# Value rows of the first token block: one-kilobyte loads put in order by 0/1 matmuls, with a new instruction order

## The chip, the cores and the metric

The kernel runs on one core of a Trainium2 chip. A core has a matrix engine (TensorE, PE in the profile; its weight loads are listed apart as PEld), three engines for elementwise work (VectorE, DVE; ScalarE, ACT; GpSimd, POOL), and SyncE (SP), which here only issues DMA transfers. The metric is the device time of one execution in microseconds. Three runs of the kernel before gave 293.53, 294.14 and 294.15 us; the median is 294.14 us.

## The reference

Attention within chunks of 64 tokens, then a bilinear feed-forward layer. q, k and v are float32 of shape (8, 8, 576, 64): batch, head, token, head dimension.

```python
def _attn_ref(q, k, v):
    B, H, S, D = q.shape                      # 8, 8, 576, 64
    chunk = 64
    q_c, k_c, v_c = (x.reshape(B, H, S // chunk, chunk, D) for x in (q, k, v))
    scores = (1.0 / np.sqrt(D)) * np.matmul(q_c, k_c.transpose(0, 1, 2, 4, 3))
    scores = scores - np.max(scores, axis=-1, keepdims=True)
    attn = np.exp(scores)
    attn = attn / (np.sum(attn, axis=-1, keepdims=True) + 1e-09)
    return np.matmul(attn, v_c).reshape(B, H, S, D)

def _moe_ref(x, w_a, w_b, w_out):             # x: 4608 tokens x 512
    a = x @ w_a                               # 512 x 1536
    b = x @ w_b
    return a * b @ w_out                      # 1536 x 512
```

Between the two, the heads of a token are joined: x is the attention's output as 4608 rows of 512.

## The kernel before

**Tiling.** The 4608 tokens are nine blocks of 512, numbered K = 0 to 8, and each block is two units of 256 tokens, u = 0 to 17. A block's attention output stands in the tile `xT` (features on partitions, tokens along the free axis). The feed-forward layer of a block multiplies `xT` with the weights `WA` and `WB` (twelve pieces `ft` of 128 columns each), multiplies the two results into `AB`, and multiplies `AB` with `WO`. From block 1 on, the two products use seven half-size products instead of eight (`side_group`, L832 and its product at L861; `out_seven`, L1135 and L1166; the last block's is `out_last`, L1004). Block 0's first product is plain (`ffn`, L762, product at L772).

**Attention of block 0.** It is done in quarters: head pairs m = 0 to 3, two heads of all 512 tokens each. `load_pair` (L364) loads q and k of one pair; partition p holds the four tokens 4p to 4p + 3 of a head one after the other, so that each contiguous run in memory is 4 x 64 float32, one kilobyte. `cast_pair` makes bf16 of it, `turn_pair` (L480, matmuls at L492) transposes it on TensorE and copies it back from PSUM in token order (`qkT`), `scores_pair` (L506, matmuls at L518, exponentials to `E` at L528), `sums_pair` (L533, matmuls with ones at L541; the inverse on DVE with a reciprocal at L551 for pair 1, on ACT as exp(-ln) at L555 and L557 for the others) and `values_pair` (L560, matmuls at L570, the multiplication with the inverse into `xT` at L583).

**v of block 0.** The value product needs v with the token on the partition. `load_v0` (L373) loads it so: four transfers, each of 128 tokens, all eight heads; a run in memory is one token of one head, 64 float32, 256 bytes. Two casts (`cast_v`, L592) turn the two float32 halves into the bf16 tiles `vb[0]` and `vb[1]`, 128 x 1024 each. All four `values_pair` wait for both casts.

**Units 2 and 3** (block 1) are loaded and turned in the same way (`TWO_UNITS`); their v comes by `load_v0(..., 1)`, in 256-byte runs. Later units are loaded in token order and turned by a DMA transpose (`turn_dma`, L602).

**Weights.** `load_four` loads 256 rows by 512 columns of `w_a` or `w_b` (512 KB, runs of two kilobytes) into one of eight staging tiles `wst`, and a cast writes them to `WA` or `WB`. There are twelve such loads, X0, X1 and X2, four each. `load_wo` does the same for `w_out`.

**Order.** Nothing is scheduled while the kernel is built. Each piece of work is an operation with a number, the engines that may do it, and what it reads and writes (`Planner.op`, L25). The text `ORDER_OF_ALL` (L85) lists all operations in one order, each with the engine that does it (a PE, b ACT, c DVE, d POOL, e SP) and, where it takes one, the PSUM bank. `follow` (L53) emits them in that order. Each engine works through its own part of the list strictly in order; only semaphores between engines tell when. Words with f are filler matmuls of zeros (L1474) that write a free bank and are read by nobody; there are 30. Transfers are issued by SP, and the k pairs of block 0 by ACT's queue, and share a set of completion semaphores, eight transfers deep: a transfer is issued when the one eight before it has landed. Some POOL operations also wait for the DVE operation listed just before them (the `turn` dependency at the end of the kernel).

## Time and profile before

| | |
|---|---|
| median of three runs | 294.14 us (293.53 to 294.15) |
| span of the profiled execution, first to last instruction | 291.4 us |
| PE busy | 285.0 us (98%), 3522 matmuls |
| DVE busy | 245.6 us (84%) |
| ACT busy | 181.5 us (62%) |
| POOL busy | 175.3 us (60%) |
| DMA | 55.09 MB in 140248 packets, mean 189 GB/s |
| first product of block 0's feed-forward layer (L772) | starts at 16.28 us |
| first product of block 1 (L861) | starts at 42.94 us |

The profile gives the span of one execution; its own device time is not given apart from that. The median of the runs is 2.7 us above the span, which is what lies before the first and after the last instruction. The profile counts matmuls with modelled ends, so that "busy" on PE also covers short waits between them; the time from the start of one group of matmuls to the start of the next tells more than their listed duration. Times in the profile are counted from the first instruction.

### The profile page before, as it was taken

How to read it: one execution, taken by the hardware profiler on the slowest of the kernel's cores; microseconds unless marked ns; L12 is line 12 of the kernel's file. 1: busy time of each engine (PE TensorE's matmuls, PEld its weight loads, DVE VectorE, ACT ScalarE, POOL GpSimd, SP SyncE). 2: the span in 40 equal slices, each digit the busy share in tenths (PEclk: the TensorE clock that was granted, in tenths of full speed). 3: DMA queues.
4: the chain of work that ended last, by engine and by line, in shares of the span. 5: the costliest groups of instructions: out<-in, count | busy, mean ns of one | idle time of the engine just before them, and what ended most of it. 6: DMA issues, size and time to landing. Idle time of an engine off the chain costs nothing.

```text
span 291.4 us, 8635 instructions
## 1 busy us (share of the span) xinstructions
PE 285.0 (98%) x3522; PEld 232.6 (80%) x3522; DVE 245.6 (84%) x432; ACT 181.5 (62%) x308; POOL 175.3 (60%) x168
## 2 busy tenths in 40 slices
PE   8999989999999999999999999999999999999995
PEld 3545448887888888888888888888888888888884
DVE  2758989999897999989998989888997788697893
ACT  1767878978877775795675468525944684333221
POOL 3354248443789389835739694569447764676540
PEclk9999999999999999999999999999999999999999
DMA  7999999999998789939996995939290210003034
GB/s 244 335 395 393 310 282 340 246 216 246 213 213 219 191 175 274 240 75 201 260 259 158 203 277 126 253 88 242 76 219 3 80 69 2 0 2 144 3 133 156
DMA packets 140248, 55.09 MB, mean 189 GB/s; under 512 B 126256, under 2 KB 131504, under 8 KB 140208
## 3 DMA queue, kind: packets, MB, share of 16 engines
q1 hardware_dynamic: 138976, 53.43, 71.8%
q10 hardware_dynamic: 1232, 1.11, 1.1%
q8 instruction: 27, 0.44, 0.7%
q14 instruction: 13, 0.11, 0.1%
HBM read 37.75 MB, written 9.44 MB: 162 GB/s over the span
## 4 chain that ended last, share of the span: by engine, by line
PE 91%; ACT 3%; DVE 2%; DMA 1%; issue 1%; POOL 0%; SPq 0%; POOLq 0%
PE F L861 49%; PE F L1166 24%; PE F L772 6%; PE F L1004 3%; PE F L1474 2%; PE F L635 1%; PE F L645 1%; PE F L492 1%; PE F L673 1%; DMA f<-in_k_dram 1%; ACT inv L697 1%; ACT inv L695 1%; DVE xT L722 0%; POOL wst L821 0%; ACT E L528 0%
## 5 line engine op out<-in xcount | busy, mean ns | idle before, releaser
L326 ACT COPY part<-F 128x512 f32<-128x512 f32 x87 | 50.4, 591 | 49.0 <-PE F L861 32.2
L895 POOL TENSOR_TENSOR AB<-AB,bsb 128x512 bf16<-128x512 bf16 x45 | 51.7, 1156 | 38.7 <-DVE wst L1123 15.5
L899 DVE TENSOR_TENSOR bsb<-F,part 128x512 bf16<-128x512 f32 x72 | 49.0, 685 | 10.4 <-PE F L861 4.9
L326 ACT COPY wst<-F 128x512 f32<-128x512 f32 (+1 forms) x43 | 24.0, 561 | 30.5 <-PE F L861 14.7
L861 PEld LDWEIGHTS <-WB 128*128 128x128 bf16 x384 | 37.3, 98 | 5.2 <-issue 0.5
L861 PEld LDWEIGHTS <-WA 128*128 128x128 bf16 x384 | 37.2, 98 | 4.8 <-issue 0.3
L899 DVE TENSOR_TENSOR AB<-F,part 128x512 bf16<-128x512 f32 x48 | 32.9, 686 | 3.7 <-PE F L861 1.6
L1123 POOL TENSOR_TENSOR wst<-AB 128x512 bf16<-128x512 bf16 x27 | 31.0, 1155 | 7.0 <-PE F L1166 4.7
L861 PEld LDWEIGHTS <-Ta 128*128 128x128 bf16 x288 | 27.9, 98 | 3.9 <-issue 0.5
L861 PEld LDWEIGHTS <-Tb 128*128 128x128 bf16 x288 | 27.4, 98 | 4.4 <-issue 0.9
L1166 PEld LDWEIGHTS <-AB 128*128 128x128 bf16 x288 | 28.0, 98 | 3.4
L1166 PEld LDWEIGHTS <-wst 128*128 128x128 bf16 x288 | 27.8, 98 | 3.4
L861 PE MATMUL F<-wst,Ta 128*128 128x256 bf16 x192 | 28.8, 273 | 0.1
L861 PE MATMUL F<-wst,Tb 128*128 128x256 bf16 x192 | 28.8, 273 | 0.0
L861 PE MATMUL F<-wst,WB 128*128 128x256 bf16 x192 | 28.8, 273 | 0.0
L861 PE MATMUL F<-wst,WA 128*128 128x256 bf16 x192 | 28.8, 273 | 0.0
L861 PE MATMUL F<-xT,WA 128*128 128x256 bf16 x192 | 28.2, 273 | 0.0
L861 PE MATMUL F<-xT,WB 128*128 128x256 bf16 x192 | 28.1, 273 | 0.0
L1166 PE MATMUL F<-WO,AB 128*128 128x256 bf16 x192 | 25.5, 273 | 0.0
L326 DVE COPY part<-F 128x512 f32<-128x512 f32 x33 | 22.4, 684 | 2.7 <-PE F L861 2.0
L326 ACT CAST qkb<-f 128x1024 bf16<-128x1024 f32 (+1 forms) x24 | 23.2, 986 | 0.3 <-DMA f<-in_q_dram 0.3
L1123 POOL TENSOR_TENSOR wst<-wst,AB 128x512 bf16<-128x512 bf16 x16 | 18.4, 1155 | 6.0 <-DVE wst L1123 5.9
(126 smaller groups left out, 551.7 us busy)
## 6 DMA issues: line engine op xcount, KB each, us to landing
f<-in_q_dram SPq DMA_DIRECT2D x32, 256.0 KB, 4.2
f<-in_v_dram SPq DMA_DIRECT2D x32, 256.0 KB, 4.2
f<-in_k_dram SPq DMA_DIRECT2D x28, 256.0 KB, 4.8
out_dram<-osb SPq DMA_DIRECT2D x28, 256.0 KB, 3.5
wst<-in_moe_w_b_dram SPq DMA_DIRECT2D x6, 512.0 KB, 7.8
wst<-in_moe_w_a_dram SPq DMA_DIRECT2D x6, 512.0 KB, 6.9
wst<-in_moe_w_out_dram SPq DMA_DIRECT2D x6, 512.0 KB, 6.8
out_dram<-osb SPq DMA_DIRECT2D x12, 128.0 KB, 2.4
```

Source lines behind the costliest of these rows:

```text
L326: return A.copy(out=out, in_=in_) if e == "act" else ENG[e].tensor_copy(out=out, in_=in_)
L492: T.transpose(turned()[:, r, :], qkb[hu][:, x, mm * 512 + r * 128:mm * 512 + r * 128 + 128], identity)
L635: T.matmul(PS[j][cl * 64:cl * 64 + 64, c:c + 64], chunk_of(u, 1, m, j, 2 * g + cl), chunk_of(u, 0, m, j, 2 * g + cl), start=True, stop=True,)
L645: T.matmul(SU[cl][j * 64:j * 64 + 64, :], ones[cl * 64:cl * 64 + 64, :], E[u % 2][cl * 64:cl * 64 + 64, j, :], start=True, stop=True,)
L772: T.matmul(f_of(b)[:, 0:n].rearrange("p (u t) -> p u t", u=len(us)), w[ft][:, kt, :], x[:, us[0]:us[-1] + 1, kt, :], start=(kt == 0), stop ...
L861: T.matmul(f_of(bank)[:, q * 256:q * 256 + 256], lhs(2 * g + q, kt), rhs[:, kt, :], start=(first and q == 0 and kt == 0), stop=(q == 1 and ...
L895: op(("dve", "pool"), TIMES, lambda e: ENG[e].tensor_tensor(out=dst, in0=dst, in1=b, op=MULT), r=bk, w=key, prio=-300, fast=True)
L899: op("dve", c_dve(512), lambda e: V.tensor_tensor(out=dst, in0=two(f_of(bank)), in1=two(pab[s][i]), op=ADD), r=[("ps", id(bank)), ("part", ...
L1004: T.matmul(f_of(bank)[:, 0:256], lhs[:, i, h], rhs[:, i, :], start=(first and i == 0), stop=(i == NP - 1), skip_group_check=True)
L1123: op(*long_op(hs), lambda e, i=i, x=x, y=y, o_=o_: ENG[e].tensor_tensor(out=SS[i][:, s], in0=x[:, s], in1=y[:, s], op=o_), r=fts + [(name, ...
L1166: T.matmul(f_of(bank)[:, at:at + 256], lhs[:, i, tt * 128:tt * 128 + 128], rhs[:, i, :], start=(first and at == 0 and i == 0), stop=(i == ...
L1474: "fn": lambda e: T.matmul(F[at], zero[:, 0:128], zero, start=True, stop=True),
```

## The change

Three things are changed.

1. `load_v0` of block 0 (`K in PLACED`) loads v by head pairs, as q and k are loaded: four transfers of 256 KB in runs of one kilobyte, four tokens on a partition.
2. `place_v` brings it into token order. For each half (four heads), two copies cast 128 x 512 float32 to bf16 into a part of the output tile `osb[0]` that is not yet in use, with the four residues r of the token index apart. Sixteen matmuls then put the rows in place: the stationary operand is a 32 x 128 piece of `picks`, a matrix of zeros with a one where column - 3 equals four times the partition, and the moving operand is a 32 x 256 piece of v. Four are accumulated over r for each of four 32-row groups g, which write four PSUM banks. Four copies of 128 x 256 bring these to `vb`. The keys of `vb` are now kept apart by half, so that pairs 0 and 1 wait for the first half only. `picks` (128 x 515 bf16, in `osb[2]`) is made at the start by a memset and a select on GpSimd. The two `cast_v` of block 0 are gone.
3. `ORDER_OF_ALL` is another table, for all operations of the kernel. It was made for three sets of transfer times. Operation numbers differ between the tables. In the new one the first weight load comes after the q, k and v loads of block 0 and three of the q and k loads of units 2 and 3 (before: none of these three), all twelve weight loads come before the v loads of units 2 and 3 (before: two of these four v loads came ahead of the last two weight loads), and there are 25 fillers.

```diff
--- before.py
+++ after.py
@@ -83,95 +83,90 @@
 ORDER_OF_ALL = """
-c113 e0 b1 e2 b3 e4 e8 b5 e6 e9 c48 f0 f1 f2 f3 f4 f5 f6 f7 f0 f1 a49:0 c50 d51 f2 a52:1 d57 f3 f4 a58:2 b7
...
+c125 e0 b1 e2 d48 b3 e4 b5 e6 d57 b51 b7 f0 f0 f0 f0 f0 f0 f0 f0 a52:0 a49:1 a58:2 b59 c60 a61:3 b62 f4 f4 f4 f4
...
 """
@@ -247,6 +242,9 @@
     SUMS_AT = 12
     EARLY_CASTS = ("pool", "act", "dve")
     TWO_CASTS = ("pool", "act", "dve")
+    PLACED = (0,)
+    BY_HALF = (0,)
+    PLACE_CASTS = ("pool", "act", "dve")
 
     sb = ctx.enter_context(tc.tile_pool(name="sb", bufs=1))
     pp = ctx.enter_context(tc.tile_pool(name="pp", bufs=1, space=bass.MemoryType.PSUM))
@@ -317,6 +315,8 @@
     TS[0] = WO[:, :, 0, 256:512]
     TW = [[W[:, 1::2, 0:2]] + [buf(f"T{x}_{i}", [128, NP, 2, 128], BF16) for i in range(3)] for x, W in (("b", WB), ("a", WA))]
 
+    picks = osb[2].rearrange("p t c -> p (t c)").bitcast(BF16)[:, 0:515]
+
     V, A, G, T, SP = nc.vector, nc.scalar, nc.gpsimd, nc.tensor, nc.sync
     P = Planner({"F": range(NF)})
     op = P.op
@@ -371,6 +371,15 @@
         ))
 
     def load_v0(half, K=0):
+        if K in PLACED:
+            for m in (2 * half, 2 * half + 1):
+                mm = m % 2
+                load(
+                    f32[half][2][:, mm * 512:mm * 512 + 512].rearrange("p (h c) -> p h c", h=2),
+                    v[K, 2 * m:2 * m + 2, 0:BLK, :].rearrange("h (p r) d -> p h (r d)", r=4),
+                    [("f32", half, 2, 2 * mm), ("f32", half, 2, 2 * mm + 1)], (256, 42),
+                )
+            return
         for n in range(2):
             g = 2 * half + n
             load(
@@ -574,7 +583,7 @@
                             start=True, stop=True,
                         )
 
-        op("pe", 0.157, pe, r=[("E", hu, mm, j) for j in range(2)] + [("vb", 0), ("vb", 1)], w=[("ps", id(x)) for x in PA], ps=PA, prio=R0 + m + 0.4, mode="64")
+        op("pe", 0.157, pe, r=[("E", hu, mm, j) for j in range(2)] + [("vb", n, g, hu) for n in range(2) for g in range(2)], w=[("ps", id(x)) for x in PA], ps=PA, prio=R0 + m + 0.4, mode="64")
         if MERGE and not mm:
             return
         a, n = (hu * 2, 2) if MERGE else (m, 1)
@@ -589,9 +598,50 @@
                    w=[("xT", 0, u, y, cl) for u in range(2) for y in range(a, a + n)], ps=[PA[cl]], prio=R0 + m + 0.4)
             o["ahead"] = AHEAD * (1 - hu)
 
+    def vb_keys(n):
+        return [("vb", n, g, h) for g in range(2) for h in range(2)]
+
     def cast_v(u, engs, prio):
         cost = {"dve": 0.69, "pool": 1.04, "act": 1.05}
-        op(engs, [cost[e] for e in engs], lambda e: copy(e, vb[u % 2], f32[u % NF32][2]), r=f_keys(u, 2), w=[("vb", u % 2)], prio=prio, fast=True)
+        op(engs, [cost[e] for e in engs], lambda e: copy(e, vb[u % 2], f32[u % NF32][2]), r=f_keys(u, 2), w=vb_keys(u % 2), prio=prio, fast=True)
+
+    def v_rows(K, half):
+        return osb[K].rearrange("p t c -> p (t c)").bitcast(BF16)[:, half * 1024:half * 1024 + 1024]
+
+    placing = {}
+
+    def place_v(K, half):
+        cost = {"dve": 0.425, "pool": 0.61, "act": 0.62}
+        rows = v_rows(K, half)
+        for mm in range(2):
+            op(PLACE_CASTS, [cost[e] for e in PLACE_CASTS], lambda e, mm=mm: copy(
+                e,
+                rows.rearrange("p (r h d) -> p r h d", r=4, h=4)[:, :, 2 * mm:2 * mm + 2],
+                f32[half][2][:, mm * 512:mm * 512 + 512].rearrange("p (h r d) -> p r h d", h=2, r=4),
+            ), r=[("f32", half, 2, 2 * mm), ("f32", half, 2, 2 * mm + 1)], w=[("osb", K, half, mm)], prio=R0, fast=True)
+        if K in BY_HALF or not half:
+            placing[K] = [P.bank("F") for _ in range(4)]
+            keep.extend(placing[K])
+        VB = placing[K]
+
+        def pe(e):
+            for r in range(4):
+                for g in range(4):
+                    T.matmul(
+                        f_of(VB[g])[:, half * 256:half * 256 + 256],
+                        picks[32 * g:32 * g + 32, 128 * g + 3 - r:128 * g + 131 - r],
+                        rows[32 * g:32 * g + 32, r * 256:r * 256 + 256],
+                        start=(r == 0), stop=(r == 3), skip_group_check=True,
+                    )
+
+        op("pe", 0.441, pe, r=[("osb", K, half, mm) for mm in range(2)] + [("osb", 2, 0, 0), ("osb", 2, 0, 1)], w=[("ps", id(b)) for b in VB], ps=VB, prio=R0, mode="32")
+        if K in BY_HALF or half:
+            for g in range(4):
+                hs = (half,) if K in BY_HALF else (0, 1)
+                c = slice(256 * hs[0], 256 * hs[-1] + 256)
+                n = 256 * len(hs)
+                op(("act", "dve"), (c_act(n), c_dve(n)), lambda e, g=g, c=c: copy(e, vb[g // 2][:, g % 2 * 512:g % 2 * 512 + 512][:, c], f_of(VB[g])[:, c]),
+                   r=[("ps", id(VB[g]))], w=[("vb", g // 2, g % 2, h) for h in hs], ps=[VB[g]], prio=R0)
 
 
     def cast_natural(u, x, engs, prio):
@@ -726,7 +776,7 @@
                     op=MULT,
                 ), r=[("ps", id(PA[cl]))] + i_keys(u), w=[("xT", (u // 2) % NX, u % 2, m, cl) for m in range(4)], ps=[PA[cl]], prio=prio)
 
-        return 0.256, lambda: mm_values(u, [f_of(x) for x in PA]), e_keys(u) + [("vb", n) for n in ((0, 1) if u in TWO else (u % 2,))], PA, old, post
+        return 0.256, lambda: mm_values(u, [f_of(x) for x in PA]), e_keys(u) + ([("vb", n, g, u % 2) for n in range(2) for g in range(2)] if u in TWO else vb_keys(u % 2)), PA, old, post
 
     def part_scores(u, prio):
         PS = P.bank("F"), P.bank("F")
@@ -1313,8 +1363,11 @@
             cast_pair(x, m, PAIR_CASTS[2 * m + x])
             turn_pair(m, x, PAIR_TURNS[2 * m + x])
         scores_pair(m)
-    cast_v(0, V_CASTS, R0 + 0.4)
-    cast_v(1, V_CASTS, R0 + 0.5)
+    for half in range(2):
+        if 0 in PLACED:
+            place_v(0, half)
+        else:
+            cast_v(half, V_CASTS, R0 + 0.4)
     for m in range(2):
         sums_pair(m)
         values_pair(m)
@@ -1343,7 +1396,9 @@
 
     def value_in(u):
 
-        if u < NU:
+        if u in TWO and 1 in PLACED:
+            place_v(1, u % 2)
+        elif u < NU:
             cast_v(u, EARLY_CASTS if u < 8 else CASTS, -60 + u)
 
     AT = -200.0
@@ -1476,6 +1531,8 @@
     with tc.manual_schedule():
         V.memset(ones, 1.0)
         make_identity(nc, identity)
+        G.memset(picks, 0.0)
+        G.affine_select(out=picks, in_=picks, pattern=[[-1, 515]], compare_op=mybir.AluOpType.not_equal, fill=1.0, base=3, channel_multiplier=4)
         tables, turn = False, None
         for o in order:
             if o["eng"] == "act" and not o["land"] and not tables:
```

171 lines of the change are left out of this document (83 added, 88 removed).

## The prediction

> **What bounds the kernel now.** I read the page first (its shares and the 40 slices), then the busy time of the dense stretch, then the chain of work that ended last, and then the timeline of the first 45 us. The page:
>
> ```profile
> span 291.4 us, 8635 instructions
> ...
> PE 285.0 (98%) x3522; PEld 232.6 (80%) x3522; DVE 245.6 (84%) x432; ACT 181.5 (62%) x308; POOL 175.3 (60%) x168
> ...
> GB/s 244 335 395 393 310 282 340 246 216 246 213 213 219 191 175 274 240 75 201 260 259 158 203 277 126 253 88 242 76 219 3 80 69 2 0 2 144 3 133 156
> ```
>
> The table of busy time by stretch, 42 to 250 us (PE busy first):
>
> ```profile
> 42.00:250.00 208.00, 207.85 (x2710) 179.65 (x2708) 186.40 (x327) 140.57 (x228) 137.32 (x124) 1.00 0.79 183
> ```
>
> PE is busy for 207.85 of 208 us. From 42 us on it sets the time, and a change gains nothing there unless it takes PE work away. Of PE work the change takes none: it adds 32 small matmuls and drops five fillers. What can move is how early the dense part starts. The chain that ended last (start, length, work):
>
> ```profile
> 16.28 5.89 PE F L772 x26
> 22.39 4.75 PE F L772 x22
> 27.14 0.67 PE F L492 x12
> ...
> 28.70 0.62 PE F L492 x8
> 29.75 0.86 PE F L772 x4
> ...
> 41.27 1.83 PE F L772 x8
> 43.11 9.61 PE F L861 x88
> ```
>
> and PE in the timeline around it:
>
> ```profile
> 35.52 2.33 PE L772 MATMUL F<-xT,WA 128*128 128x512 bf16 x10
> 38.69 1.47 PE L772 MATMUL F<-xT,WA 128*128 128x512 bf16 x6 [0.83 <-DVE WA L326]
> 40.54 0.73 PE L660 MATMUL F<-E,vb 64*64 64x64 bf16 x64 [0.38 <-DVE vb L326]
> ...
> 42.94 0.60 PE L861 MATMUL F<-xT,WB 128*128 128x256 bf16 x4
> ```
>
> From the first L772 to the first L861 pass 42.94 - 16.28 = 26.66 us. A 512-column product costs 4.75 / 22 = 0.216 us, so the first 26 lose 5.89 - 5.61 = 0.28; the ten at 35.52 should end at 37.68, yet the next starts at 38.69 (1.01 lost, for the weight cast); those six should end at 39.99, yet 40.54 follows (0.55, for the v cast of unit 2). The eight transposing products at 28.70 take 8 x 0.67 / 12 = 0.45 and not 0.62, and four more (0.22) fill only half of the way from 29.32 to 29.75: 0.38. That is **2.2 us of gaps and 24.45 of work**. So three numbers decide: the start of L772 (16.28), this work, these gaps.
>
> **The transfers.** Rows of the timeline whose idle time ended with a landing, and SP's rows:
>
> ```profile
> 4.10 0.43 DVE L326 CAST qkb<-f 128x512 bf16<-128x512 f32 x1 [2.89 <-DMA f<-in_q_dram]
> ...
> 5.52 1.17 POOL L326 CAST qkb<-f 128x512 bf16<-128x512 f32 x2 [0.32 <-DMA f<-in_q_dram]
> ...
> 7.15 1.17 POOL L326 CAST qkb<-f 128x512 bf16<-128x512 f32 x2 [0.46 <-DMA f<-in_q_dram]
> ...
> 12.46 1.04 POOL L326 CAST vb<-f 128x1024 bf16<-128x1024 f32 x1 [3.31 <-DVE vb L326]
> ...
> 14.38 1.04 POOL L326 CAST WB<-wst 128x1024 bf16<-128x1024 f32 x1 [0.88 <-DMA wst<-in_moe_w_b_dram]
> ...
> 15.65 1.04 POOL L326 CAST WA<-wst 128x1024 bf16<-128x1024 f32 x1 [0.24 <-DMA wst<-in_moe_w_a_dram]
> ...
> 28.66 3.66 SPq L355 DMA_DIRECT2D wst<-in_moe_w_a_dram  x2
> ...
> 37.93 0.69 DVE L326 CAST WA<-wst 128x1024 bf16<-128x1024 f32 x1 [1.18 <-DMA wst<-in_moe_w_a_dram]
> ```
>
> Rates by stretch (last column GB/s): pairs in 1 KB runs, v in 256-byte runs mixed with other loads, weights:
>
> ```profile
> 5.00:7.50 2.50, 2.50 (x18) 1.62 (x17) 1.26 (x2) 0.00 (x0) 1.72 (x4) 1.00 1.11 356
> 10.50:13.40 2.90, 2.70 (x37) 1.24 (x36) 2.90 (x3) 2.49 (x7) 0.94 (x1) 1.00 1.12 325
> 16.00:23.00 7.00, 6.98 (x62) 3.38 (x50) 3.37 (x8) 4.28 (x8) 3.33 (x4) 1.00 1.06 396
> ```
>
> At 356 to 396 GB/s a 256 KB pair takes 0.66 to 0.74 us; a weight load took 15.65 - 14.38 = 1.27. In the new order q of pair 3 follows q and k of pair 2 (7.15) at about 8.0; the four v and three pairs of units 2 and 3 follow until about 13.0; the first weights land at about 14.4 and 15.7, as before, since three more loads (2.0 us) stand against v at the faster rate (four loads at about 0.25 less) and against SP no longer held by v's issues. The last weights come without two v loads ahead of them and without SP's 3.66 us stall: after 15.7 follow five pairs and ten weight loads, 5 x 0.7 + 10 x 1.27 = 16.2, so about 32 us against 37.9. That gain lies beside PE's work, and only the 1.01 gap of the 2.2 is its direct worth.
>
> **Start of L772: the chain for v.** Durations:
>
> ```profile
> 0.73 0.20 POOL masks.py:197 MEMSET identity<- 128x128 bf16 x1 [0.29 <-POOLq L1510]
> ...
> 1.01 0.29 POOL masks.py:199 TENSOR_SCALAR_AFFINE_SELECT identity<-identity 128x128 bf16<-128x128 bf16 x1
> ...
> 6.17 2.11 DVE L326 COPY qkT<-F 128x512 bf16<-128x512 bf16 x3 [1.65 <-PE F L492]
> ...
> 9.71 0.36 PE L541 MATMUL F<-E,ones 64*64 64x256 bf16 x4
> 10.09 1.76 DVE L551 RECIPROCAL inv<-F 128x256 f32<-128x256 f32 x1
> 11.98 0.62 ACT L326 CAST qkb<-f 128x512 bf16<-128x512 f32 x1
> 12.49 0.40 ACT L555 ACTIVATE inv<-F 128x256 f32<-128x256 f32 x1
> 14.58 1.64 DVE L583 TENSOR_TENSOR xT<-F,inv 128x256 bf16<-128x256 f32 x4 [0.53 <-ACT inv L555]
> ```
>
> Removed are two casts of v (1.04 on POOL; the other, on DVE, of the same size: the WA cast above, 0.69). Added are four casts of 128 x 512 (two on POOL, two on DVE at 0.43), two placings on PE, eight copies of 128 x 256 (five on ACT at up to 0.40, three on DVE at 0.41, the L583 share). `picks` has four times the identity's columns, so POOL spends up to 4 x 0.49 = 2.0 on it from 1.3 us on; it has nothing else to do before q and k land (4.1 us and after), and without that cover the first cast would be late by as much. A placing is 16 products of 256 columns: four 32-row groups side by side would take 4 x 0.11 = 0.44, all in a row 16 x 0.11 = 1.75; four 64-row products of 256 columns took 0.36 together, less than 4 x 0.11, so side by side; I take 0.55 with its end.
>
> The new list puts on DVE, in this order: the reciprocal for pair 1, the two casts of v, one copy of half 0, the second reciprocal, two copies of half 1, a copy of unit 3's transpose, and the four multiplications into `xT` for pairs 0 and 1, which L772 needs. PE's product for the first reciprocal stands behind the transpose of q's pair 3. So: q at 8.0; POOL, after its two casts from 7.15 (to 8.32) and one of 0.6, 8.9; transpose and sums 0.8, 9.7; reciprocal 1.76, 11.5; cast 0.43, 11.9; placing 0.55, 12.5; copy 0.41, 12.9; reciprocal 1.75, 14.7 (half 1 is placed on PE meanwhile); two copies 0.82, 15.5; transpose copy 0.6 (of 2.11 for three, the last two follow at that pace), 16.1; four multiplications 1.64, 17.8. With a few tenths of semaphores I take **17.9, 1.6 later than 16.28**. Bounds: 17.2 if q lands half a microsecond earlier and nothing is lost between; 19.1 with products in a row in half 0. The weights (cast by 16.0) are not what it waits for. Nothing here is worth v's faster transfer: v lands by 12 us in both kernels.
>
> **Work from there to L861.** PE moves three transposes of units 2 and 3 ahead of L772 (four products of 0.67 / 12 = 0.056 each): -0.67. One filler stays inside, +0.2. Scores and sums of units 2 and 3 stand together before and apart after:
>
> ```profile
> 34.96 0.63 PE L645 MATMUL F<-E,ones 64*64 64x512 bf16 x8
> ...
> 66.44 0.41 PE L645 MATMUL F<-E,ones 64*64 64x512 bf16 x4
> ```
>
> 2 x 0.41 - 0.63 = 0.19 for sums, half that for scores: +0.3. So 24.45 - 0.2 = 24.3.
>
> **Gaps.** With the weights early, 1.01 goes. Late next is DVE: its list from the first block-0 copy to the v cast of unit 2 holds 29 instructions against 27, some 16 us in both at 0.4 to 0.7 each, but PE starts that stretch later and does less in it. The wait for the v cast (0.55) stays or grows. I take 0.9; bounds 0.3 and 1.5. After L861 the PE work is the same; I take 0, bounds -0.3 (the 0.15 us that PE idles from 42 to 250, and small waits) and +2 (below).
>
> **Sum.** 1.6 - 0.2 - (2.2 - 0.9) = +0.1: span 291.5. The runs' median lies 2.7 above the profiled span, so **294.2 us**. No change, as far as 0.2% (0.6 us), about what this measurement can tell, goes.
>
> **Rivals.**
>
> *Slower: TensorE's clock falls back.* Fillers and the first products:
>
> ```profile
> 1.26 4.45 PE L1474 MATMUL F<-zero 128*128 128x512 bf16 x10 [1.26 <-DVE zero L1271]
> ...
> 6.73 0.59 PE L1474 MATMUL F<-zero 128*128 128x512 bf16 x2
> ...
> 15.12 0.38 PE L1474 MATMUL F<-zero 128*128 128x512 bf16 x1
> ```
>
> The first ten took 0.44 each, later ones 0.21 (0.59 less the 0.38 that one alone takes): half speed until some 6 us. Before, fillers ran until 15.1 us. In the new list, from the second placing (about 14.5) to 17.9 stand three transposes, one sums and four values products and no filler, some 1.7 us of work in 3.4. If that lets the clock fall, the first L772 run at 0.43 for as long as the ten did, 4.5 us, and lose half, 2.2; a shorter slow stretch loses less. I price it at 1.8: 296.0. Against it: by the walk above PE is never idle for two microseconds at a stretch. The Trainium skill (TensorE: Matmul & The Clock Gate, Part 1) says that the array falls to half clock after an idle window of about 3.4 us; by that rule, with no such idle window in the list, the clock holds, and were it to fall, one window at half rate would lose 1.7 us, an estimate from that page.
>
> *Slower: a transposed unit is late.* From the list of transfers:
>
> ```profile
> qkT<-qkb SPq DMA_TRANSPOSE x14, 4.1
> ```
>
> Before, the last q or k cast of any unit after 3 stands at least 9 us of PE work ahead of that unit's scores. In the new list unit 4 has 6.9 and unit 9 has 4.9, against a cast of 1.04 and a transfer of 4.1 to landing, 5.1. It decides from the point at which POOL's or SP's queue holds that cast or transfer more than about a microsecond. Price 1 to 2 us: 295.7.
>
> *Faster: the chain for v is shorter and the gaps vanish.* If q's pair 3 lands early and the queues hold no lag, L772 starts at 17.2 and runs without any gap with all weights ahead of it: 0.9 - 0.2 - 2.0 = -1.3, 292.9. For it: the weights' lead of 6 us. Against it: every term must go well.
>
> *The transfer is hidden anyway* is part of my sum: the 1 KB runs give no time of their own.
>
> **How the numbers follow.** Forecast 0.42 (own range 293.5 to 295.0: the start and gaps within half their bounds), faster rival 0.23, clock 0.12, late unit 0.23. Of the forecast's 0.42, 0.20 lie within 0.6 us, 0.12 below, 0.10 above; the slower rivals give 0.32 above and 0.03 within. So faster 0.35, same 0.23, slower 0.42. The range takes in the rivals: low 292.6, high 296.6.
>
> **What would show it.** L772 starts at 17.9 (17.2 to 19.1), after DVE's second reciprocal and four multiplications, not after a weight cast; the last weight cast waits for a landing near 32; L861 starts within 0.5 us of 42.94; PE from there is busy as before; L772's first products take 0.22. Wrong it would be by L861 starting early with PE gaps gone, by slow L772, or by PE waiting for `qkT` near 62 or 120 us.

## The result, and the profile after

The changed kernel takes 292.76 us (median of 18 runs, 292.43 to 294.81) against 293.72 us for the kernel before on the same chip (18 runs, 292.84 to 294.51): ratio 0.9972, 95% interval 0.9959 to 0.9984. It is about 0.3% faster; the prediction said no change, 294.2.

The profile page of the changed kernel, its span and busy times:

```profile
span 290.7 us, 8704 instructions
...
PE 285.5 (98%) x3549; PEld 233.4 (80%) x3549; DVE 246.2 (85%) x433; ACT 176.2 (61%) x307; POOL 185.9 (64%) x180
```

The table of busy time by stretch, for the dense part (PE busy first) and for the stretch from the first ffn product, now L822, to the first side product, now L911:

```profile
42.00:250.00 208.00, 208.00 (x2714) 180.38 (x2713) 187.37 (x324) 131.46 (x220) 148.55 (x135) 1.00 0.79 181
...
17.58:42.38 24.80, 24.80 (x254) 11.79 (x255) 21.19 (x39) 20.49 (x34) 7.38 (x8) 1.00 1.05 342
```

The same stretch of the kernel before, from its first L772 to its first L861:

```profile
16.28:42.94 26.66, 25.39 (x264) 12.08 (x265) 20.95 (x36) 20.46 (x36) 10.32 (x13) 1.00 1.01 344
```

So PE starts 17.58 - 16.28 = 1.30 us later, and needs 26.66 - 24.80 = 1.86 us less from there. The first side product comes 0.56 earlier, 42.38 against 42.94. From there to the end of the span pass 290.7 - 42.38 = 248.32 us against 291.4 - 42.94 = 248.46: the 0.15 that PE idled in the dense part is gone too. Sum 0.70, which is the difference of the spans.

PE's rows in the timeline after, from the first ffn product on:

```profile
17.58 2.00 PE L822 MATMUL F<-xT,WB 128*128 128x512 bf16 x8
...
35.75 2.76 PE L822 MATMUL F<-xT,WA 128*128 128x512 bf16 x12
38.45 0.41 PE L695 MATMUL F<-E,ones 64*64 64x512 bf16 x4
38.79 1.04 PE L822 MATMUL F<-xT,WA 128*128 128x512 bf16 x4
39.66 0.38 PE L1529 MATMUL F<-zero 128*128 128x512 bf16 x1
39.97 0.74 PE L710 MATMUL F<-E,vb 64*64 64x64 bf16 x64
...
42.38 0.60 PE L911 MATMUL F<-xT,WB 128*128 128x256 bf16 x4
```

The twelve products at 35.75 answer to the ten and six at 35.52 and 38.69 of before: there is no wait between them for a weight cast. Of the wait for v only 0.31 is left, and a filler covers it (39.66 to 39.97).

The timeline ahead of L822, engine by engine; a bracket tells the idle time before a row and what ended it:

```profile
9.81 1.75 DVE L560 RECIPROCAL inv<-F 128x256 f32<-128x256 f32 x1
10.82 1.67 PE L1529 MATMUL F<-zero 128*128 128x512 bf16 x7
11.48 0.69 DVE L326 CAST osb<-f 128x512 bf16<-128x512 f32 x2
12.43 0.62 PE L630 MATMUL F<-osb,osb 32*128 32x256 bf16 x16
13.48 1.75 DVE L560 RECIPROCAL inv<-F 128x256 f32<-128x256 f32 x1
15.98 1.04 POOL L326 CAST WB<-wst 128x1024 bf16<-128x1024 f32 x1 [1.46 <-DMA wst<-in_moe_w_b_dram]
16.45 1.41 DVE L592 TENSOR_TENSOR xT<-F,inv 128x256 bf16<-128x256 f32 x4
17.22 1.04 POOL L326 CAST WA<-wst 128x1024 bf16<-128x1024 f32 x1 [0.20 <-DMA wst<-in_moe_w_a_dram]
```

L822 stands behind the reciprocals, the placing and the four multiplications, as forecast: its first product starts when the third multiplication has ended (17.53), its second when the fourth has (17.86). The first weight cast, though, ends at 17.02, only half a microsecond earlier.

One more thing about the numbers: each run also gives the span of its execution. For the kernel before these lie between 291.3 and 293.7 (29 executions beside the first experiments, median 292.2), so that its profiled 291.4 is one of its best. The time of each of these 29 executions is 1.74 to 1.85 us above its own span: the 2.7 us of the table ahead of the change are not what lies outside the span, but set a median time against the span of a good execution. For the changed kernel the spans lie between 290.6 and 292.3 with a median of 290.75: its profiled 290.7 is a usual one. The times below are therefore read by ratios, and the traces for where the time stands.

### The profile page after: what moved, and what is told of

Same layout as the page of the kernel before. It is cut to its first block, busy times and chain, and to the rows that moved or that the text cites. A ratio compares the mean times of both kernels' runs of the same rounds, so it can differ in the third digit from the quotient of the medians.

```text
span 290.7 us, 8704 instructions
## 1 busy us (share of the span) xinstructions
PE 285.5 (98%) x3549; PEld 233.4 (80%) x3549; DVE 246.2 (85%) x433; ACT 176.2 (61%) x307; POOL 185.9 (64%) x180
## 4 chain that ended last, share of the span: by engine, by line
PE 95%; DMA 3%; DVE 0%; POOL 0%; issue 0%; ACT 0%; ACTq 0%
PE F L911 51%; PE F L1216 25%; PE F L822 7%; DMA f<-in_k_dram 3%; PE F L1054 3%; PE F L685 2%; PE F L723 2%; PE F L695 2%; PE F L1529 1%; PE F L501 1%; PE F L630 0%; PE F L579 0%; PE F L673 0%; PE F L550 0%; PE F L710 0%; POOL qkb L326 0%
## 5 line engine op out<-in xcount | busy, mean ns | idle before, releaser
L326 ACT COPY part<-F 128x512 f32<-128x512 f32 x91 | 52.5, 591 | 52.0 <-PE F L911 36.2
L945 POOL TENSOR_TENSOR AB<-AB,bsb 128x512 bf16<-128x512 bf16 x46 | 52.8, 1155 | 21.0 <-DVE wst L1173 7.2
L1173 POOL TENSOR_TENSOR wst<-AB 128x512 bf16<-128x512 bf16 x30 | 34.3, 1155 | 13.4 <-PE F L1216 9.9
L911 PEld LDWEIGHTS <-WA 128*128 128x128 bf16 x384 | 37.1, 98 | 5.5 <-issue 1.1
L911 PEld LDWEIGHTS <-WB 128*128 128x128 bf16 x384 | 37.6, 98 | 4.6
L326 ACT COPY wst<-F 128x512 f32<-128x512 f32 (+1 forms) x40 | 22.1, 557 | 29.7 <-PE F L1216 17.9
L911 PEld LDWEIGHTS <-Tb 128*128 128x128 bf16 x288 | 27.6, 98 | 3.9 <-issue 0.5
L911 PEld LDWEIGHTS <-Ta 128*128 128x128 bf16 x288 | 27.7, 98 | 3.6 <-issue 0.3
L911 PE MATMUL F<-wst,Tb 128*128 128x256 bf16 x192 | 28.9, 273 | 0.0
L911 PE MATMUL F<-wst,Ta 128*128 128x256 bf16 x192 | 28.9, 273 | 0.0
L911 PE MATMUL F<-xT,WA 128*128 128x256 bf16 x192 | 28.9, 273 | 0.0
L911 PE MATMUL F<-wst,WA 128*128 128x256 bf16 x192 | 28.8, 273 | 0.0
L911 PE MATMUL F<-wst,WB 128*128 128x256 bf16 x192 | 28.8, 273 | 0.0
L911 PE MATMUL F<-xT,WB 128*128 128x256 bf16 x192 | 28.3, 273 | 0.0
L326 POOL CAST qkb<-f 128x1024 bf16<-128x1024 f32 (+1 forms) x21 | 17.2, 835 | 15.1 <-DVE Tb L859 6.3
L1216 PE MATMUL F<-WO,AB 128*128 128x256 bf16 x192 | 24.6, 273 | 0.0
L326 DVE COPY part<-F 128x512 f32<-128x512 f32 x29 | 19.8, 686 | 2.7 <-PE F L911 2.3
L772 DVE TENSOR_TENSOR xT<-F,inv 128x512 bf16<-128x512 f32 x28 | 18.0, 684 | 2.6 <-ACT inv L747 2.1
```

Of the source, the lines that this page charges most:

```text
L326: return A.copy(out=out, in_=in_) if e == "act" else ENG[e].tensor_copy(out=out, in_=in_)
L772: op("dve", c_dve(512), lambda e, cl=cl: V.tensor_tensor(out=x.rearrange("p m (g c t) -> p c g m t", g=2, c=2)[:, cl], in0=f_of(PA[cl]).re ...
L911: T.matmul(f_of(bank)[:, q * 256:q * 256 + 256], lhs(2 * g + q, kt), rhs[:, kt, :], start=(first and q == 0 and kt == 0), stop=(q == 1 and ...
L945: op(("dve", "pool"), TIMES, lambda e: ENG[e].tensor_tensor(out=dst, in0=dst, in1=b, op=MULT), r=bk, w=key, prio=-300, fast=True)
L1173: op(*long_op(hs), lambda e, i=i, x=x, y=y, o_=o_: ENG[e].tensor_tensor(out=SS[i][:, s], in0=x[:, s], in1=y[:, s], op=o_), r=fts + [(name, ...
L1216: T.matmul(f_of(bank)[:, at:at + 256], lhs[:, i, tt * 128:tt * 128 + 128], rhs[:, i, :], start=(first and at == 0 and i == 0), stop=(i == ...
```

## The experiments

All ratios are to the kernel before, timed on the same chip; the changed kernel stands at 0.9972. Each run has 6 to 18 executions, on one of several chips; the kernel before has a median span of 292.0 to 292.3 beside each of the experiments. The runs in which only v's run length is changed, and the one with a quarter of the placing, use v in a wrong order or in part: they price a part of the kernel and could not be used in its place.

| run | ratio | 95% interval | spans: lowest, median | first ffn product | first side product |
|---|---|---|---|---|---|
| changed kernel | 0.9972 | 0.9959 to 0.9984 | 290.6, 290.75 | 17.58 | 42.38 |
| before, weights ahead of v | 0.9971 | 0.9955 to 0.9987 | 290.8, 291.5 | 16.48 | 42.47 |
| before, v in 1 KB runs | 0.9925 | 0.9903 to 0.9947 | 289.7, 290.3 | 15.46 | 42.22 |
| before, both | 0.992 | 0.989 to 0.995 | 289.3, 289.85 | 16.16 | 42.23 |
| changed, v in 256-byte runs | 0.9992 | 0.9971 to 1.0012 | 291.0, 292.05 | 17.89 | 42.67 |
| changed, block 1 in 1 KB runs | 0.9969 | 0.9953 to 0.9985 | 290.7, 291.0 | 18.70 | 43.49 |
| changed, weights behind v | 1.0056 | 1.0028 to 1.0084 | 291.7, 293.35 | 17.79 | 46.45 |
| the same with fillers | 1.0051 | 1.0031 to 1.0071 | 292.9, 293.9 | 17.57 | 44.52 |
| changed, a quarter of the placing | 0.9937 | 0.9913 to 0.9962 | 290.3, 290.5 | 17.18 | 41.97 |
| changed, reciprocals on ACT | 0.9985 | 0.9958 to 1.0012 | 291.1, 291.4 | 16.50 | 43.15 |
| the same, head reordered | 1.002 | 1.0006 to 1.0034 | 292.5, 292.6 | 16.15 | 44.21 |
| changed, v cast early | 0.9955 | 0.9937 to 0.9974 | 290.5, 290.7 | 17.57 | 42.15 |
| changed, no fillers | 0.9986 | 0.9968 to 1.0005 | 290.8, 292.0 | 18.26 | 43.85 |

### Which part of the gain is the order of the loads, which the run length?

The kernel before, SP's words of its table alone:

```diff
-e26 e137 e138 e32 e34 e119 e118 e36
+e26 e32 e34 e137 e138 e119 e118 e36
```

> The kernel before, with one thing moved in SP's list: the last two loads of weights (wa) are issued ahead of all four loads of v of block 1, not between them. The computation is whole. Theory (the gain of the change is the order of transfers): in the kernel before, the wa load issued at 28.66 stands behind two v loads in 256-byte runs, the next is issued only at 31.90, and the last two weights land at 35.25 and 37.91 (2.66 apart, where 1.27 is a weight's pace). With both ahead of v they should land near 33 and 34.3, the last v near 38 in place of 39.58, and both the 1.01 us ahead of the product at 38.69 and most of the 0.55 ahead of the values product at 40.54 should go: first side product 1.0 to 1.5 us earlier than 42.94, time 0.3 to 0.5% below the kernel before. Rival (the order is worth nothing, the faster v transfers made the lead): no difference, since v's last landing then stays at 39.6 and the values product at 40.5.

The order alone gives as much as the whole change, 0.9971. PE in the timeline of this run:

```profile
35.84 3.63 PE L772 MATMUL F<-xT,WA 128*128 128x512 bf16 x16
40.06 0.74 PE L660 MATMUL F<-E,vb 64*64 64x64 bf16 x64 [0.59 <-DVE vb L326]
...
42.47 0.60 PE L861 MATMUL F<-xT,WB 128*128 128x256 bf16 x4
```

The sixteen products that a weight cast had cut at 38.69 run through. The wait for the v cast stays, which is why the first side product gains 0.47 and not 1.0 or more.

The run length alone, in the load of v in the kernel before:

```diff
-f32[half][2][:, n * 512:(n + 1) * 512].rearrange("p (h d) -> p h d", h=H),
-v[K, :, g * 128:(g + 1) * 128, :].transpose([1, 0, 2]),
+f32[half][2][:, n * 512:(n + 1) * 512].rearrange("p (h d) -> p h d", h=H if K else 2),
+v[K, :, g * 128:(g + 1) * 128, :].transpose([1, 0, 2]) if K else v[K, 2 * g:2 * g + 2, 0:BLK, :].rearrange("h (p r) d -> p h (r d)", r=4),
```

> The kernel before, with only v of block 0 fetched in 1 KB runs by pairs of heads, into the same buffers, with the old table; nothing puts it in token order, so v of block 0 is used in a wrong order and the output is not the reference's. It prices the faster transfer by itself. Theory (the stream of transfers, 0.25 us less for each of four loads, is ahead of PE everywhere up to 40 us): everything behind v lands 0.9 us earlier, L772 starts at 16.0 to 16.3 as before (reciprocals and multiplications on DVE), the gap at 38.69 shrinks from 1.01 to about 0.1 and the values product starts 0.9 earlier; time 0.2 to 0.3% below the kernel before. Rival (as predicted: the 1 KB runs give no time of their own): within 0.1% of before, with the weights' landings earlier but the gaps as they were.

SP's rows of the kernel before, and a stretch of its table by time (last column GB/s):

```profile
4.81 4.51 SPq L355 DMA_DIRECT2D f<-in_v_dram  x3
9.36 0.82 SPq L355 DMA_DIRECT2D wst<-in_moe_w_b_dram  x1
...
9.00:12.00 3.00, 2.97 (x47) 1.57 (x44) 2.60 (x3) 1.87 (x7) 0.14 (x1) 1.00 1.26 295
```

The same of this run, and its PE:

```profile
4.77 1.88 SPq L355 DMA_DIRECT2D f<-in_v_dram  x3
7.29 0.37 SPq L355 DMA_DIRECT2D wst<-in_moe_w_b_dram  x1
...
9.00:12.00 3.00, 2.80 (x41) 1.34 (x41) 3.00 (x4) 1.96 (x6) 0.51 (x2) 1.00 1.08 398
...
15.46 1.46 PE L772 MATMUL F<-xT,WB 128*128 128x512 bf16 x6
...
37.96 1.47 PE L772 MATMUL F<-xT,WA 128*128 128x512 bf16 x6 [1.05 <-DVE WA L326]
```

Two things get faster: the stream moves 398 GB/s and not 295, and SP, which three loads in 256-byte runs held for 4.51 us, is through with them in 1.88, so that the first weight load is issued 2.07 us earlier. The theory had the start stay and the gap close. It is the other way round: the gap stays (1.05 ahead of 37.96), but all of PE's work stands 0.7 to 0.8 us earlier in this trace, and the time falls by 0.75%. The rival, which was the prediction's premise, is refuted. The Trainium skill (DMA: Bandwidth & Descriptors, Specifications) asks for at least 512 bytes a transfer for the full rate; these two rates agree with that.

Both together:

> The kernel before with both single steps: v of block 0 in 1 KB runs (no placing, so v is used in a wrong order and the output is not the reference's) and the last two weight loads issued ahead of v of block 1. It shows what the transfers are worth without the price of the placing. Theory (two separate terms, the rate of v and the order of the last loads): L772 starts at 15.5 as with the 1 KB runs alone, the gap of about 1 us ahead of the ten products near 37 is gone and so is most of the wait for the v cast; first side product at 41.2 to 41.6, against 42.94 before, 42.47 with the order alone and 42.22 with the runs alone; span about 289.8, time 0.2 to 0.4% below the kernel with the runs alone. Rival (both act on the same wait, so the second adds nothing): first side product at 42.2, time as with the runs alone.

The ratio is 0.992, no different from 0.9925. The first side product, expected at 41.2 to 41.6, comes at 42.23. The trace has sixteen products in a row from 35.66 and a wait of 0.54 for the v cast, as with the order alone, but starts at 16.16 and not at 15.46, though both kernels issue the same up to 24 us. So the first transfers differ between two executions by some 0.7 us, and one trace each can't add up these terms. That the second step adds little is what the ratios say, within 0.4%.

The other way round, the changed kernel with its v loads in 256-byte runs again (placing and table kept):

```diff
-f32[half][2][:, mm * 512:mm * 512 + 512].rearrange("p (h c) -> p h c", h=2),
-v[K, 2 * m:2 * m + 2, 0:BLK, :].rearrange("h (p r) d -> p h (r d)", r=4),
+f32[half][2][:, mm * 512:mm * 512 + 512].rearrange("p (h d) -> p h d", h=H),
+v[K, :, m * 128:(m + 1) * 128, :].transpose([1, 0, 2]),
```

> The changed kernel, with only v of block 0 fetched again in 256-byte runs, everything else (placing, table) as it is; the rows then stand in a wrong order and the output is not the reference's. Theory (the faster transfer is a term of its own): v's last landing goes from 11.92 to about 12.8, the first weights from 15.92 to about 16.8, L822 starts 0.4 to 0.9 later than 17.58 (its first weight cast ended at 17.02, so 0.4 of the delay is covered), and every later weight is 0.9 late against a slack of about 0.4: time 0.4 to 0.9 us (0.15 to 0.3%) above the changed kernel. Rival (the transfer is hidden): same time as the changed kernel, start at 17.6.

SP's row of the changed kernel, then SP and PE of this run:

```profile
2.76 3.39 SPq L355 DMA_DIRECT2D f<-in_v_dram  x3
...
2.76 4.90 SPq L355 DMA_DIRECT2D f<-in_v_dram  x3
...
17.89 2.00 PE L822 MATMUL F<-xT,WB 128*128 128x512 bf16 x8
...
42.67 0.60 PE L911 MATMUL F<-xT,WB 128*128 128x256 bf16 x4
```

In the trace it costs 0.3 us, though the last load of v lands 0.9 us later (12.83 against 11.92). In the times the whole gain is gone, 0.9992, with an interval that overlaps the changed kernel's. The twelve executions have spans of 291.0 to 293.5 with a median of 292.05, against 290.75 for the changed kernel; ten of them are at 291.3 or above, and four of the changed kernel's 18. The short runs cost 1.3 us in the median and 0.4 in the best execution. Where in the kernel the slower executions lose the rest, one trace cannot show.

And v of block 1 in 1 KB runs, where nothing waits for the stream:

> The changed kernel with v of block 1 fetched in 1 KB runs too, into the same buffers and with nothing that puts it in token order, so v of block 1 is used in a wrong order and the output is not the reference's. It asks whether the faster transfer is worth its time wherever it stands or only where PE waits for the stream. Theory (worth only at the head): the last v lands at about 36.3 in place of 37.29 and SP is not held for 3.09 and 3.24 us at 26.84 and 29.97, but the v casts stand behind other work on ACT and DVE (37.39 and 39.16), so the values product stays near 39.97, the first side product near 42.38, and the time within 0.1% of the changed kernel. Rival (the stream sets the pace to the end of the stretch and beyond): first side product 0.3 to 1.0 us earlier and the time with it.

The ratio is 0.9969, the changed kernel's own. The profiled execution is a late one: it starts at 18.70, though the two kernels are the same up to 26 us, and from there needs 43.49 - 18.70 = 24.79, as the changed kernel. The run length is worth its time at the head, and nothing that these intervals could show in block 1.

### Do the weights' lead and the clock matter?

The changed kernel, SP's words again:

```diff
-e30 e32 e34 e150 e149 e130 e131
+e30 e150 e149 e32 e34 e130 e131
```

> The changed kernel, with the first two loads of v of block 1 issued ahead of the last two weight loads, as the kernel before has them. The computation is whole. Theory (the lead of the weights over v is what closed the gaps): the last weights land at about 35 and 37.5 in place of 32.05 and 33.33, PE, which takes up their products at 35.75, waits 1 to 2 us, the start stays at 17.58; time 0.8 to 2 us (0.3 to 0.7%) above the changed kernel, that is at or above the kernel before. Rival (the gaps were closed by something else, such as v's run length or the fewer products in the stretch): the weights late by under 1 us and no wait over 0.3 us on PE, same time as the changed kernel.

```profile
35.95 0.60 PE L822 MATMUL F<-xT,WA 128*128 128x512 bf16 x2
38.51 4.08 PE L822 MATMUL F<-xT,WA 128*128 128x512 bf16 x10 [1.95 <-ACT WA L326]
...
38.50:42.50 4.00, 3.97 (x10) 1.25 (x10) 3.24 (x6) 2.85 (x5) 1.16 (x1) 0.57 1.03 253
```

As expected the wait is back, 1.95 us, and the kernel is slower than before. But the first side product comes 4.1 us later than in the changed kernel and not 2: after the wait ten products take 0.41 each, and the column of the granted clock (the third from the right) has 0.57 for these four microseconds. Four of the twelve executions show a mean clock of 0.994, and they are the four slowest (296.54 to 297.22 us); the other eight take 293.6 to 296.3. The profiled one is of the four.

With ten fillers on PE ahead of the waiting products (`a213`):

```diff
-a239:46 c265 a213:7
+a239:46 c265 f7 f7 f7 f7 f7 f7 f7 f7 f7 f7 a213:7
```

> The changed kernel with the last weights late, as in the run before, and ten filler products (0.22 us each at full clock) put on PE ahead of the products that wait for the last weight cast. The computation is whole. In the run without fillers PE stood idle 2.1 us ahead of 38.51 and the next ten products then took 0.41 us each, a granted clock of 0.57 from 38.5 to 42.5. Theory (the wait itself costs 2 us and the clock that falls back after it as much again): with PE busy until about 38.2 the ten products take 0.22 each again, the first side product comes near 44.7 in place of 46.45, time 1.5 to 2 us (0.5 to 0.7%) below the run without fillers and 1 to 2.5 us above the changed kernel. Rival (the slow products have another cause, such as reading a weight tile that is being written): they still take about 0.4 each, same time as without fillers.

```profile
35.74 2.33 PE L1529 MATMUL F<-zero 128*128 128x512 bf16 x9
37.91 2.75 PE L822 MATMUL F<-xT,WA 128*128 128x512 bf16 x12
```

Twelve products take 2.75, the full rate, and no execution shows a clock under 0.999: the slow products came of the idle PE and not of the weight tile. The first side product comes at 44.52, as expected. The time is the same, though (1.0051): the fillers, there in every execution, take as long as the wait, and the fallback that they prevent came in four of twelve only. As a measure of what the fallback costs the run is inconclusive.

The fillers ahead of L822, taken out of the changed kernel between `c84` and `a182`:

```diff
-c84 f3 f3 f3 f3 f3 f3 f3 a86:3501
+c84 a86:3501
...
-a81:62 f7 a111:71 b112 b82 f3 f3 f3 a93:3057
+a81:62 a111:71 b112 b82 a93:3057
```

> The changed kernel without the eleven fillers between 10.8 and 14.6 us (ahead of L822); the computation is whole. It tests the rival of the prediction that PE's clock falls back ahead of L822. PE then does about 4.4 us of work in the 7.6 us from 9.9 to 17.5, and its longest idle stretch is about 1.4 us (11.0 to 12.4). Theory (the clock falls back only behind an idle stretch of about 2 us, as ahead of the late weights, where 4 of 12 executions showed a mean granted clock of 0.994): start and time as in the changed kernel, first products of L822 at 0.22 each, granted clock 0.998 to 1.0 in all executions. Rival (a sparse stretch is enough): the first products take 0.4 each in some or all executions and the time is 1 to 2 us above the changed kernel in these.

```profile
10.98 0.40 PE L501 MATMUL F<-identity,qkb 128*128 128x128 bf16 x4 [0.51 <-POOL qkb L326]
12.04 0.62 PE L630 MATMUL F<-osb,osb 32*128 32x256 bf16 x16 [0.66 <-DVE osb L326]
...
18.26 2.81 PE L822 MATMUL F<-xT,WB 128*128 128x512 bf16 x8
...
10.00:13.00 3.00, 1.82 (x54) 1.04 (x54) 2.49 (x4) 2.68 (x9) 1.88 (x4) 1.00 1.10 388
14.00:17.50 3.50, 3.50 (x66) 2.15 (x64) 3.32 (x8) 2.58 (x8) 2.67 (x4) 0.50 1.06 397
```

My theory was wrong. PE's longest idle stretch there is 0.66 us, yet behind three microseconds in which it was busy for 1.82 the granted clock is 0.50 until after 17.5. DVE's four multiplications end at 17.87, as in the changed kernel, but PE at half clock comes to L822 only at 18.26, and takes 25.59 us from there to the first side product and not 24.80. Eight of twelve executions show a mean clock of 0.988 to 0.994; the median of the spans is 292.0 against the changed kernel's 290.75. By the ratio half of the gain is gone, though the intervals overlap. So the fillers, which the new table still has, kept the prediction's clock rival off in most executions: in the changed kernel one of 18, the slowest (294.81), shows 0.994.

### What sets the start of L822?

The placing with a quarter of its products (`for r in range(1)`, each closed by itself):

> The changed kernel with a quarter of the placing products: of each 16 only the four of the first row group position are made, so most of v's rows are missing and the output is not the reference's; casts, copies and table stay. It prices the products that put v in order. Theory (the chain for v on DVE sets the start): each placing takes about 0.2 in place of 0.62, the copies of half 0 and the second reciprocal come 0.4 earlier, and L822 starts at 17.1 to 17.2, where the first weight cast, done at 17.02, becomes what it waits for; time 0.3 to 0.45 us (0.1 to 0.15%) below the changed kernel. Rival (the weights already set the start): L822 still at 17.5 to 17.6, same time.

```profile
17.18 2.00 PE L822 MATMUL F<-xT,WB 128*128 128x512 bf16 x8
...
41.97 0.60 PE L911 MATMUL F<-xT,WB 128*128 128x256 bf16 x4
...
117.50 0.44 PE L685 MATMUL F<-qkT 64*64 64x64 bf16 x32 [0.26 <-DMA qkT<-qkb]
```

The start moves by 0.40 and the first side product by 0.41: the chain for v set the start, and the earlier start is handed on in full to there. The span of this execution, though, is 290.7, the changed kernel's. The scores at 117.50 wait for a transposed tile to land; in the changed kernel they stand at 117.57, without a wait. An earlier start thus runs into the next limit, the late transposed unit that the prediction had as a rival. The ratio goes from 0.9972 to 0.9937, with intervals that just overlap, and the median of the spans from 290.75 to 290.5. The price of these 24 products is thus 0.4 us at the start, about half of what the run length alone gains in its trace; how much of it the whole kernel pays, these times tell only roughly.

The reciprocals on ACT, the first weights earlier, three transposes later (numbers of the changed kernel's table). The new table also has six fillers and not eleven between 10.8 us and L822:

```diff
-    RECIP = (1,)
+    RECIP = ()
...
-e10 e145 e128 e12 e16 e14 e148 e18 e127 e129 e20 e22
+e10 e12 e16 e14 e18 e145 e128 e148 e127 e20 e129 e22
...
-a93 a152 a102 a118 a139 a108 a133 a115 a122 a182
+a93 a102 a108 a111 a118 a115 a122 a182
```

> The changed kernel with a shorter head; the computation is whole. The sums of pair 1 are inverted on ACT by Ln and Exp as the other pairs' are, not by two reciprocals of 1.75 us on DVE; the first four weight loads go ahead of three loads of q and k of block 1; three transposes of block 1 stand behind the first sixteen products of the ffn and not ahead of them. Theory (what sets the start of L822 is DVE's chain, reciprocals above all, and next the first weights): L822 starts at 16.0 to 16.6 in place of 17.58, PE's stretch to the first side product is 0.3 to 0.7 longer than 24.80, first side product at 41.2 to 41.9, time 0.5 to 1.2 us (0.2 to 0.4%) below the changed kernel. Rival (the stream of transfers sets the end of the stretch, not its start): L822 starts early but PE then waits for weights or for casts on ACT and DVE, and the first side product stays within 0.3 of 42.38.

```profile
16.50 1.90 PE L822 MATMUL F<-xT,WB 128*128 128x512 bf16 x8
...
20.88 1.20 ACT L326 CAST qkb<-f 128x512 bf16<-128x512 f32 x2 [3.09 <-DMA f<-in_k_dram]
...
23.89 0.83 PE L501 MATMUL F<-identity,qkb 128*128 128x128 bf16 x12 [0.73 <-ACT bsb L326]
...
43.15 0.60 PE L911 MATMUL F<-xT,WB 128*128 128x256 bf16 x4
```

The start came as expected, 1.08 earlier; as several things were changed at once, it does not tell which of them held it. The stretch took 26.65 and not 24.80. Three transposes that cost PE no time ahead of L822 now stand in it (0.67), and ACT, in its fixed order, waited 3.09 for a load of block 1 while a cast of block 0 stood behind it. One of the twelve executions, 297.29 us, has a mean clock of 0.988. A second try took these casts off ACT and moved weights and ffn work ahead:

> The short head of the run with the sums of pair 1 inverted on ACT, with what held PE there moved out of the way; the computation is whole. In that run L822 started at 16.50, yet PE waited 0.73 us near 23.9 for a cast of block 0's ffn that stood on ACT behind two casts of block 1 which waited for loads (ACT idle 3.09 us ahead of 20.88), DVE waited 2.26 us ahead of 23.55 in the same way, and the first side product came at 43.15. Here those two casts go to POOL, the ffn's casts and products stand ahead of the late transposes on ACT and DVE, two weight loads go ahead of three pair loads, the scores of unit 2 stand behind one more group of products, the v cast of unit 2 stands two places earlier on DVE and the filler at 39.66 is left out. Theory (the start is worth its full size as soon as no engine's list holds the stretch): start 16.4 to 16.7, first side product 41.4 to 42.0 against 42.38, time 0.3 to 1.0 us below the changed kernel. Rival (the engines beside PE are full in the stretch, so an earlier start is given back): first side product at 42.3 or later, time as the changed kernel or above.

```profile
24.50 0.83 PE L501 MATMUL F<-identity,qkb 128*128 128x128 bf16 x8 [1.03 <-POOL qkb L326]
...
26.44 1.04 PE L822 MATMUL F<-xT,WB 128*128 128x512 bf16 x4 [0.45 <-POOL WB L326]
...
44.21 0.60 PE L911 MATMUL F<-xT,WB 128*128 128x256 bf16 x4
```

Worse: with the pairs of block 1 behind the weights, their casts come late on POOL, and PE waits for them. The start at 16.15 is given back twice over. In neither try could the earlier start be had alone.

### What is left of the gaps?

DVE's cast of v for unit 2 ahead of two multiplications, the filler left out:

```diff
-c199 c207 e131 e274 c144 c215
+e131 c144 c199 c207 e274 c215
...
-f0 a236:02
+a236:02
```

> The changed kernel with one instruction moved: DVE casts v of unit 2 ahead of two multiplications of the ffn and not behind them, and the filler (39.66 to 39.97) that covered PE's wait for it is left out. The computation is whole. It prices what is left of the gaps. Theory (0.3 us of gap is left at that place in the changed kernel): the values product starts at 39.66 in place of 39.97, first side product at 42.1, time 0.3 us (0.1%) below the changed kernel. Rival (the values product waits for something else too, such as the multiplication's release of its bank): no difference.

```profile
39.74 0.74 PE L710 MATMUL F<-E,vb 64*64 64x64 bf16 x64
...
42.15 0.60 PE L911 MATMUL F<-xT,WB 128*128 128x256 bf16 x4
```

The values product starts 0.23 earlier and so does the first side product. The ratio, 0.9955, is the best of the kernels that do the whole work, but its interval and the changed kernel's overlap, and the medians of the spans are alike (290.7 and 290.75): not told apart by the times.

## Why the prediction was wrong

**The start of the ffn products.** The mechanism was right, and the size nearly: 17.58, forecast 17.9. The walk along DVE holds in its ends (first reciprocal ends at 11.56, forecast 11.5; the four multiplications at 17.86, forecast 17.8), but two errors within it nearly cancel, which is luck. The second reciprocal ends at 15.23, 0.5 later than forecast: DVE's cast of half 0 is done at 11.84, as forecast, but the placing starts only at 12.43, behind the seven fillers that stand ahead of it on PE (in the run without fillers it starts at 12.04). The four multiplications then take 1.41 and not 1.64, and DVE's instructions overlap a little. And L822 does not wait for the last multiplication, as the sum had it, but for the third.

**The first weights.** They landed at 15.92 and 17.16, not at 14.4 and 15.7. The loads ahead of them came as forecast: the last of them landed at 13.24, forecast about 13.0. But the first weight load took 2.68 us from there, where 1.27 was its pace. In the run without fillers, which has the same list of loads, it landed at 14.77, 1.29 behind. Why it differs is not shown. The chain for v covered it.

**Work and gaps.** Forecast 24.3 + 0.9 = 25.2, measured 24.80, which leaves 0.5 for gaps if the work was right. The 1.01 for the weight cast went as forecast, and the run with the weights late shows that it comes back with the order. The term that was mis-sized is the rest: "The wait for the v cast (0.55) stays or grows". It shrank to 0.31, of which 0.23 could still be had.

**After the first side product.** Forecast 0 (bounds -0.3 to +2), measured -0.14.

**The step that failed.** It is the term that was put at nothing: "Nothing here is worth v's faster transfer" and "the 1 KB runs give no time of their own". Alone the 1 KB runs make the kernel before 0.75% faster, and without them the changed kernel stands at 0.9992, which is the "no change" of the forecast. I had looked at when v lands, which is 12 us in both, and not at what stands behind v on SP and in the stream: in the kernel before, three loads in 256-byte runs held SP for 4.51 us, against 1.88 in 1 KB runs, and with it every load behind them. The prediction had both facts (SP's rows, the rates by stretch) and counted them off against three more loads. Of what the run length gives the changed kernel, the traces place 0.3 us (first side product 42.38 against 42.67); the rest shows only in how the executions spread.

**From span to time.** The prediction added 2.7 us to its span, as in the runs shown of before. For the changed kernel it is 292.76 - 290.7 = 2.06. An execution of the kernel before takes about 1.8 us more than its own span, so 0.9 of the 2.7 came from a profiled execution that was better than the median. The changed kernel's executions vary less, and with 256-byte runs they vary again. Of the miss of 294.2 - 292.76 = 1.4 us, 0.8 stands in the span (291.5 against 290.7) and 0.6 here.

**The rivals.** The faster one is what happened in kind, with a start between its 17.2 and the forecast's 17.9 and gaps of about 0.5 us in place of 2.2. That its 292.9 meets the measured 292.76 is luck: it stands for a span of 290.2, where 290.7 was measured, and the 2.7 us make up the difference. Its reason, the weights' lead, is borne out by the run with the weights late; the run length was not in it. The clock fell back in one execution of 18; the run without fillers shows how near it was. The transposed unit was not late: PE is busy for 208.00 of 208 us from 42 to 250. But it is the next limit, as the wait at 117.50 in the run with a quarter of the placing shows.

**What stays open.** The two terms, order and run length, gave 0.3% and 0.75% alone and 0.8% together; whether the second adds nothing or a few tenths of a microsecond is within the intervals. The changed kernel has both and stands at 0.9972, where the kernel before with both stands at 0.992: of this 0.5% the placing's products account for some 0.35% by the ratio, and the copies, the casts and the rest of the table were not priced one by one. Why executions with the short runs vary more was not looked into.

## What to carry to other kernels

A transfer that lands in time can still cost: look at what its issue holds up on the queue and what stands behind it in the stream, and price that by an experiment in which only the run length differs. Fillers on PE can be needed where no long idle stretch is to be seen: here a stretch in which it was busy for 1.82 of 3 us, ahead of dense work, was enough for the clock to fall. But they cost time where they stand ahead of work that is ready. When a start is moved earlier, look for the next thing that will hold the work. Before a span is turned into a time, look at how the spans of single executions lie about the profiled one.

## What the hardware showed that was not expected

The clock falls back sooner than I thought. One idle stretch of 1.95 us was enough in 4 of 12 executions, and in 8 of 12 it was three microseconds with PE busy for 1.82 and, in the trace, no idle stretch over 0.66. In the two profiled executions half the clock was granted for about 3.4 us (38.5 to 41.9) and 6.8 us (13.3 to 20.1). The Trainium skill (TensorE: Matmul & The Clock Gate, Part 1) gives the fall to half rate after at least one idle window of about 3.4 us, and calls the window free-running. That both runs fell without an idle stretch of that length differs from it, and the measurement decides; that not every execution falls agrees with a free-running window.

Loads in 256-byte runs cost twice: in rate (280 to 320 GB/s from 9 to 12 us in three traces, where three with 1 KB runs move 383 to 398) and in time on the issuing queue (4.51 us for three loads against 1.88). And the first transfers of kernels that issue the same loads at the head land at different times from one execution to the next: the first weight load at 15.92 in the changed kernel, at 16.84 in the run with block 1 in 1 KB runs, where L822 started at 18.70 and not at 17.58.
